# First modulation columns of an adaLN block: product rows with a transpose, or product columns directly

## The chip, the cores and the metric

The kernel runs on one core of one Trainium2 chip. The metric is the device time of one execution in microseconds. Three runs of the kernel before took 1825.55, 1825.82 and 1824.29 us: median 1825.55. Engines are named as in the profile: PE is TensorE's products and PEld its weight loads, DVE is VectorE, ACT is ScalarE, POOL is GpSimd, SP is the engine that issues most DMAs.

## The reference, cut to what matters

A vector `c` of 576 numbers makes six modulation rows of 576 each; the first two (`sa`, `ca`) shift and scale the normalised input ahead of the attention projections. Only that head is touched here.

```python
mod = (_silu(c) @ w_mod).reshape(c.shape[0], 6, 1, -1)
sa, ca, ga, sb, cb, gb = (mod[:, 0], mod[:, 1], mod[:, 2], mod[:, 3], mod[:, 4], mod[:, 5])
h = _layernorm(x, axis=-1) * (1 + ca) + sa
x = x + ga * _A_ref(h, A_wq, A_wk, A_wv, A_wo, A_beta)   # q, k, v = h @ wq, h @ wk, h @ wv; 4 segments of 512 tokens
h = _layernorm(x, axis=-1) * (1 + cb) + sb
x = x + gb * _B_ref(h, B_w_gate, B_w_up, B_w_down)       # SwiGLU, 4608 wide
```

Here x is 2048 x 576, in float32; the attention has 32 heads of 18 and a memory that is carried from segment to segment.

## The kernel before

The kernel works in stages: projections of the four segments of 512 tokens (with the first attention units between them), attention with its output product, and the feed-forward part, which takes about two thirds of the time. In the first stage the order on each engine is set by the scheduler of the tile framework, which may move independent instructions past each other; instructions wrapped in `pin` keep their program order among themselves. From the attention on the order is written out by hand. Every engine works through its own queue in order.

What happens first, all in the first 20 us:

- SP issues the loads: the last 64 rows of the two slices of `w_mod` (`wm[4]`, line 354), then `wm[0]` to `wm[3]` (128 rows each of both slices, line 359) between the four row blocks of the first segment of x (line 311), then four tiles of `wqk` (`wraw`, line 320).
- ScalarE and VectorE make silu(c) as columns (`sga`, lines 362 to 365). VectorE normalises the row blocks of x (lines 251 to 258), with POOL taking the power of the variance.
- The 576 values of c stand in `sga` as four columns of 128 and two of 64 (column 4 holds its values on partitions 0 to 63, column 5 on partitions 64 to 127, and `wm[4]` holds the rows for `ca` on the lower and for `sa` on the upper partitions).
- TensorE makes the two modulation rows (line 380). The stationary operand is `sgb`, each column of `sga` copied 32 times (line 372); the moving operand is a piece of 320 columns of the slice. Four products, one for each half of `ca` and of `sa`, go to four groups of 32 partitions of one bank `pr` and accumulate over the five slices.
- ScalarE takes `pr` out as `row` and adds 1 to the partitions of `ca` (line 383, by the bias `half`). TensorE turns `row` in three transposes into `pc` (line 388, `pcr` in the profile), and VectorE copies its columns to `colv` (lines 392, 393): 128 features x 5 blocks x (scale, shift).
- In between TensorE transposes the normalised x into two banks `pt` (line 263, through `trans_x`), four transposes of 128x128 for each block of 128 features.
- For each of five blocks ScalarE takes `pt` out with scale and shift from `colv`, once rounded (`hh`, line 270) and once in full (`hf`, line 271), and VectorE makes the remainder `hl` (line 272). `hr` holds both for the last 64 features.
- The first three tiles of `wqk` are split by ScalarE (`wqkh`, line 325) and VectorE (`wqkl`, line 326), the others by POOL and VectorE (lines 90, 91).
- TensorE multiplies the first three tiles by `hh`, `hl` and `hr` (`proj3`, line 559, result `pp`), then the others (line 113). ScalarE takes `pp` out (`pf`, `fh`, lines 573, 574), and the keys are transposed for the memory (line 530, `ptk`).
- ScalarE also issues the load of `gat` (line 628), on which its next step waits (line 636).

The lines that lead from `colv` to the first projection:

```python
nc.scalar.activation(hi, pt[:n], AF.Identity, scale=sc[:n], bias=bi[:n])
nc.scalar.activation(f[:n], pt[:n], AF.Identity, scale=sc[:n], bias=bi[:n])
nc.vector.tensor_tensor(lo, f[:n], f32(hi), op=ALU.subtract)
...
for kt, _ in enumerate(trans_in(0)):
    if kt == 0:
        split_qk(2)
...
for kt, t in [(kt, t) for kt in range(3) for t in QKORD[:3]] + [(kt, t) for t in QKORD[:3] for kt in (3, 4)]:
    h, l = wqkh[:, t, kt, :], wqkl[:, t, kt, :]
    for a, b in ((h, hh[kt]), (l, hh[kt]), (h, hl[kt])) if kt < 4 else ((h, hr), (l, hr)):
        nc.tensor.matmul(first[t], lhsT=a, rhs=b, start=(kt == 0 and a is h and b is hh[0]),
                         stop=(kt == 4 and a is l))
```

The constants: `ident` is the 128x128 identity, `ones` is all ones, and `tri` (128x512, made by POOL, line 152) is 0 in its first 384 columns.

Of the kernel before, what the change touches and what calls it, by code (L numbers as in the profile page):

```python
# [7 lines left out]
F32 = mybir.dt.float32  # L8
F32R = mybir.dt.float32r
BF16 = mybir.dt.bfloat16  # L10
AF = mybir.ActivationFunctionType
ALU = mybir.AluOpType
# [3 lines left out]
P = 128  # L16
# [6 lines left out]
L = 512  # L23
# [60 lines left out]
def block(ctx: ExitStack, tc: tile.TileContext, x, wqk, wv, wo, beta, wgu, wgr, wd, c, crow, w_mod, w_mod0, w_mod1, w_modc, xt, out):  # L84
    nc = tc.nc
    def pool(stk, name, bufs=1, **kw):
        return stk.enter_context(tc.tile_pool(name=name, bufs=bufs, reuse_waits="tile", **kw))
# [5 lines left out]
    def chain(*g):  # L93
        for a in g:
            yield from a

    def once(g):
        yield next(g)
# [20 lines left out]
    ident = cst.tile([P, P], F32, tag="ident", name="ident")  # L119
# [3 lines left out]
    ones = cst.tile([P, P], F32, tag="ones", name="ones")  # L123
# [3 lines left out]
    half = cst.tile([P, 1], F32, tag="half", name="half")  # L127
# [22 lines left out]
    tri = vst.tile([P, L], F32, tag="tri", name="tri")  # L150
# [3 lines left out]
    colv = cst.tile([P, 5, 2], F32, tag="colv", name="colv")  # L154
# [90 lines left out]
    def ln_stats(wk, xs, n):  # L245
        st = wk.tile([P, n, 2, 6], F32, tag=f"st{n}", name="st")
        mv = wk.tile([P, n, 2], F32, tag=f"mv{n}", name="mv")
        rs = wk.tile([P, n], F32, tag=f"rs{n}", name="rs")
        for i in range(n):
            for h in range(2):  # L250
                nc.vector.bn_stats(st[:, i, h, :], xs[i][:, 288 * h:288 * h + 288])
            nc.vector.bn_aggr(mv[:, i, :], st[:, i, :, :])
        nc.vector.tensor_scalar(rs, mv[:, :, 1], EPS, None, op0=ALU.add)
        nc.gpsimd.tensor_tensor(rs, rs, mhalf[:, :n], op=ALU.pow)
        return mv, rs

    def xhat(dst, src, mv, rs, i):
        nc.vector.tensor_scalar(dst, src, mv[:, i, 0:1], rs[:, i:i + 1], op0=ALU.subtract, op1=ALU.mult)
# [15 lines left out]
    with ExitStack() as p1:  # L274
# [5 lines left out]
        wk = pool(p1, "wk1", 2)  # L280
        ps = pool(p1, "ps1", 2, space=PSUM)
# [25 lines left out]
        def load_x(s):  # L307
            t = xs[s] = x1.tile([P, 5 * L], F32, tag="x", name=f"x{s}")[:, :4 * D].rearrange("p (a b) -> p a b", b=D)
            for i in range(4):
                r = L * s + P * i  # L310
                nc.sync.dma_start(t[:, i, :], x[r:r + P, :])
                yield
# [5 lines left out]
        def load_qk(t):  # L318
            rq[t] = raw.tile([P, 5, P], F32, tag="wraw", name="wraw", bufs=4)
            nc.sync.dma_start(rq[t], wqk[t])  # L320
# [21 lines left out]
        def trans_x(s, pts, kt, pin):  # L342
            pts[kt] = ps.tile([P, L], F32, tag="t", name="pt")
            for i in transpose_group(pts[kt], lambda i: xs[s][:, i, :], kt):
                pin(i)

        sga = wk.tile([P, 12], F32, tag="sg", name="sg")
        sg = sga[0:96, 6:12]
        with ExitStack() as p0:
            m0 = pool(p0, "m0")  # L350
            wm = {}
            gx = load_x(0)
            wm[4] = m0.tile([P, D], F32, tag="wm4", name="wm4")
            nc.sync.dma_start(wm[4], w_mod1)
            for k in range(4):
                wm[k] = m0.tile([P, 2, D], F32, tag=f"wm{k}", name=f"wm{k}")
                for _ in range(XP[k]):
                    next(gx)
                nc.sync.dma_start(wm[k], w_mod0[k])
            load_qk(0)  # L360

            nc.scalar.activation(sga, cs, AF.Exp, scale=-1.0)
            nc.vector.tensor_scalar(sga, sga, 1.0, None, op0=ALU.add)
            nc.vector.reciprocal(sga, sga)
            nc.vector.tensor_tensor(sga, sga, cs, op=ALU.mult)

            for i in range(4):
                mv, rs = ln_stats(wk, [xs[0][:, i, :]], 1)
                xhat(xs[0][:, i, :], xs[0][:, i, :], mv, rs, 0)

            sgb = wk.tile([P, 6, 32], F32, tag="sgb", name="sgb", bufs=1)
            nc.vector.tensor_copy(sgb, sga[:, 0:6].unsqueeze(2).to_broadcast([P, 6, 32]))
            pr = ps.tile([P, L], F32, tag="s1", name="pr", bufs=3)
            pin = tc.keep_in_program_order
            pt0 = {}
            for k in (4, 0, 1, 2, 3):
                for g in range(4):
                    c0 = 256 * (g % 2)
                    w = wm[4][:, c0:c0 + 320] if k == 4 else wm[k][:, g // 2, c0:c0 + 320]
                    pin(nc.tensor.matmul(pr[32 * g:32 * g + 32, :320], lhsT=sgb[:, k + g // 2 if k == 4 else k, :], rhs=w,  # L380
                                         start=(k == 4), stop=(k == 3)))
            row = wk.tile([P, L], F32, tag="hf", name="row")[:, :320]
            nc.scalar.activation(row, pr[:, :320], AF.Identity, bias=half)
            trans_x(0, pt0, 0, pin)
            pc = ps.tile([P, 3, P], F32, tag="s1", name="pcr", bufs=3)
            for b in range(3):
                n = P if b < 2 else 64
                pin(nc.tensor.transpose(pc[:n, b, :], row[:, 128 * b:128 * b + n], ident))
            trans_x(0, pt0, 1, pin)
            pv = pc.rearrange("p b (s h z) -> p b s h z", s=2, h=2)  # L390
            for h in range(2):
                nc.vector.tensor_copy(colv[:, 2 * h:2 * h + 2, :], pv[:, 0:2, :, h, 0])
            nc.vector.tensor_copy(colv[0:64, 4, :], pv[0:64, 2, :, 1, 0])

        pb = pool(p1, "pb", 2)
        pk = pb.tile([P, 4, D], F32, tag="pk", name="pk", bufs=1)
# [232 lines left out]
        for s in range(NSEG):  # L629
            if s == 0:  # L630
                gp, gw = prep(1), load_wv()
                g = chain(once(gp), once(gw), once(gp), once(gw), once(gp), gw, gp)
            else:
                g = prep(s + 1) if s + 1 < NSEG else iter(())
# [52 lines left out]
    wk = pool(p2, "wk2", 2)  # L687
    opl_ = pool(p2, "op2")
    ps = pool(p2, "ps2", 2, space=PSUM)
# [92 lines left out]
    op = pool(p2r, "op", side="right")  # L782
# [696 lines left out]
    with tc.manual_schedule():  # L1479
# [7 lines left out]
        for u in range(NU + 1):  # L1487
            s, q = divmod(u, 8)
# [25 lines left out]
        ps = pool(p2r, "pst", 2, space=PSUM)  # L1514
# [38 lines left out]
        for i in range(4):  # L1553
            for h in range(2):
                for c in range(WC):
                    n = 8 * i + 4 * h + c
# [28 lines left out]
        ps = pool(p4, "ps4", 1, space=PSUM)  # L1585
# [5 lines left out]
        n, nw = 0, PF  # L1591
# [5 lines left out]
        for t in range(2):  # L1597
            for p in range(NPR):
# [18 lines left out]
                for k in range(14):  # L1617
                    z, m = ZM[k]
# [188 lines left out]
```

## Time and profile before

| | |
|---|---|
| median of three runs | 1825.55 us |
| the profiled execution | 1824.92 us |
| its span, from the first to the last instruction | 1823.2 us |
| mean granted TensorE clock | 0.999 |
| TensorE busy (PE) | 1792.0 us, 98% |
| TensorE weight loads (PEld) | 1522.1 us, 83% |
| VectorE, ScalarE, POOL busy | 81%, 60%, 37% |

Rows of the timeline begin with the start and the duration in microseconds from the span's start; then come the engine, the line, the operation, out<-in, the size, and how many like it were merged into the row. Brackets hold the engine's idle time before it and what ended it. Rows by stretch give the stretch, its length, and each engine's busy time with its instructions. A float32 product stands in the trace as two records, since its operand is split.

### The profile page before, as it was taken

How to read it: one execution, taken by the hardware profiler on the slowest of the kernel's cores; microseconds unless marked ns; L12 is line 12 of the kernel's file. 1: busy time of each engine (PE TensorE's matmuls, PEld its weight loads, DVE VectorE, ACT ScalarE, POOL GpSimd, SP SyncE). 2: the span in 40 equal slices, each digit the busy share in tenths (PEclk: the TensorE clock that was granted, in tenths of full speed). 3: DMA queues.
4: the chain of work that ended last, by engine and by line, in shares of the span. 5: the costliest groups of instructions: out<-in, count | busy, mean ns of one | idle time of the engine just before them, and what ended most of it. 6: DMA issues, size and time to landing. Idle time of an engine off the chain costs nothing.

```text
span 1823.2 us, 31453 instructions
## 1 busy us (share of the span) xinstructions
PE 1792.0 (98%) x10627; PEld 1522.1 (83%) x10627; DVE 1481.7 (81%) x3365; ACT 1086.9 (60%) x2374; POOL 674.1 (37%) x1107
## 2 busy tenths in 40 slices
PE   7999999999999999999999999999999999999999
PEld 4888866777777788888888888888888888888888
DVE  7556388888885799889889889868888888888886
ACT  4333288878775567777777777534544544544542
POOL 2444077775466665756656656300000000000000
PEclk9999999999999999999999999999999999999999
DMA  8768766667556656355455455494333334324331
GB/s 273 258 230 281 258 209 199 194 199 227 166 164 224 209 168 193 128 176 183 134 177 184 115 165 155 154 307 153 107 107 117 96 101 129 103 83 129 107 102 53
DMA packets 146419, 306.26 MB, mean 168 GB/s; under 512 B 30964, under 2 KB 61812, under 8 KB 144468
## 3 DMA queue, kind: packets, MB, share of 16 engines
q1 hardware_dynamic: 135076, 260.19, 46.9%
q10 hardware_dynamic: 11184, 44.07, 6.2%
q8 instruction: 85, 1.39, 0.3%
q14 instruction: 74, 0.61, 0.1%
HBM read 198.69 MB, written 104.94 MB: 167 GB/s over the span
## 4 chain that ended last, share of the span: by engine, by line
PE 84%; DMA 2%; DVE 2%; ACT 2%; POOL 1%; issue 1%; SPq 0%; ACTq 0%; DVEq 0%; POOLq 0%
PE A L1321 24%; PE pd L1440 19%; PE C L1321 12%; PE B L1321 6%; PE av L731 4%; PE s L210 3%; PE s L707 3%; PE pw L841 3%; PE pd L1460 3%; PE pp L113 2%; PE pv L113 2%; PE pn L909 1%; DVE junk L215 1%; PE px L752 1%; ACT Pt L714 1%
## 5 line engine op out<-in xcount | busy, mean ns | idle before, releaser
L1321 PE MATMUL A<-y,wh 128*128 128x512 f32 x1152 | 405.1, 392 | 4.5 <-ACT tb L1350 2.0
L1448 DVE TENSOR_TENSOR acc<-acc,pd 128x576 f32<-128x576 f32 x327 | 245.0, 750 | 78.6 <-PE pd L1440 72.5
L215 DVE CUSTOM_DVE_ANT_0 junk<-s,tri 128x256 bf16<-128x256 f32 (+3 forms) x512 | 221.4, 484 | 60.8 <-PE s L210 46.7
L1440 PE MATMUL pd<-dh,ah 128*128 128x288 f32 x896 | 267.6, 299 | 0.0
L1440 PE MATMUL pd<-dl,ah 128*128 128x288 f32 x896 | 263.9, 295 | 0.0
L1440 PE MATMUL pd<-dh,al 128*128 128x288 f32 x896 | 262.5, 293 | 0.0
L1321 PEld LDWEIGHTS A<-y,wh 128*128 128x128 f32 x1152 | 216.6, 188 | 43.9 <-ACT tb L1350 2.5
L1283 DVE TENSOR_TENSOR wl<-O,wh 128x256 fp32r<-128x256 f32 x504 | 239.1, 478 | 5.5 <-ACT wh L1282 4.8
L1321 PE MATMUL A<-y,wl 128*128 128x512 f32 x576 | 225.0, 391 | 0.0
L714 ACT ACTIVATE Pt<-s 128x512 f32<-128x512 f32 (+1 forms) x352 | 182.7, 558 | 44.3 <-PE s L707 28.0
L1321 PE MATMUL C<-y,wh 128*128 128x512 f32 x576 | 202.7, 393 | 0.0
L1282 ACT CAST wh<-O 128x256 fp32r<-128x256 f32 x504 | 198.2, 405 | 4.4 <-DMA O<-in_wgu_dram 2.5
L1440 PEld LDWEIGHTS pd<-dh,ah 128*128 128x128 f32 x896 | 168.4, 188 | 18.5 <-ACT pd L1416 3.9
L1440 PEld LDWEIGHTS pd<-dl,ah 128*128 128x128 f32 x896 | 169.7, 189 | 16.2
L1386 DVE TENSOR_TENSOR al<-sg,ah 128x512 fp32r<-128x512 f32 x240 | 177.1, 738 | 6.8 <-ACT ah L1385 6.5
L1276 POOL TENSOR_TENSOR O<-O 128x128 f32<-128x128 f32 x280 | 156.4, 592 | 69.8 <-DMA O<-in_wgu_dram 40.9
L1440 PEld LDWEIGHTS pd<-dh,al 128*128 128x128 f32 x896 | 169.2, 189 | 0.0
L1385 ACT CAST ah<-sg 128x512 fp32r<-128x512 f32 x240 | 149.0, 621 | 26.3 <-DVE sg L1345 25.6
L707 PE MATMUL s<-qs,ks 110*128 110x512 f32 (+2 forms) x384 | 143.2, 390 | 4.1 <-ACT Pt L714 1.8
L210 PE MATMUL s<-ks,qs 108*128 108x256 f32 (+3 forms) x512 | 143.8, 334 | 2.6 <-DVE mx L215 2.5
L1321 PEld LDWEIGHTS C<-y,wh 128*128 128x128 f32 x576 | 108.0, 188 | 18.8
L1321 PEld LDWEIGHTS A<-y,wl 128*128 128x128 f32 x576 | 108.3, 188 | 14.9
(389 smaller groups left out, 4063.5 us busy)
## 6 DMA issues: line engine op xcount, KB each, us to landing
wr<-rD SPq DMA_DIRECT2D x216, 112.0 KB
O<-in_wgu_dram SPq DMA_DIRECT2D x36, 512.0 KB
oD<-O ACTq DMA_DIRECT2D x36, 512.0 KB
O<-oD SPq DMA_DIRECT2D x36, 512.0 KB
ks<-kD SPq DMA_DIRECT2D x96, 144.0 KB
O<-in_wgu_dram SPq DMA_DIRECT2D x36, 384.0 KB
qs<-qD SPq DMA_DIRECT2D x64, 192.0 KB
y<-yD SPq DMA_DIRECT2D x11, 1024.0 KB
```

What stands on the lines that cost most here:

```text
L210: nc.tensor.matmul(bank[:, n * (h - h0):n * (h - h0) + n], lhsT=qst[b][0:108, h, 128 * i:128 * i + 128], rhs=kst[b][0:108, h // 2, 0:n], s ...
L215: nc.vector.tensor_tensor_reduce(junk[:, :n], bank[:, n * (h - h0):n * (h - h0) + n], tri[:, L - n:], 1.0, -3e38, op0=ALU.add, op1=ALU.max ...
L707: nc.tensor.matmul(bank[:, n * (g - h):n * (g - h + w)].rearrange("p (a b) -> p a b", a=w), lhsT=kst[u % NB][0:110, g // 2, 128 * j:128 * ...
L714: nc.scalar.activation(pt[:, h:h + per, :n], bank[:, :n * per].rearrange("p (a b) -> p a b", a=per), AF.Exp, scale=SCALE)
L1276: eng.tensor_tensor(o[:, d, i, s_], o[:, a, i, s_], o[:, b, i, s_], op=op)
L1282: nc.scalar.copy(wh, o)
L1283: later.append(lambda: nc.vector.tensor_tensor(wl, o, f32(wh), op=ALU.subtract))
L1321: nc.tensor.matmul(bank, lhsT=a, rhs=b, start=(first and n == 0), stop=(n == 6), skip_group_check=not first)
L1385: nc.scalar.copy(ah, src)
L1386: later.append(lambda: nc.vector.tensor_tensor(al, src, f32(ah), op=ALU.subtract))
L1440: nc.tensor.matmul(pd[:, i, :288], lhsT=a[:, tk], rhs=w, start=(add and k == 0), stop=(k == 2), skip_group_check=not add)
L1448: nc.vector.tensor_tensor(o, o, pd[:, :, :288], op=ALU.add)
```

## The change

The slices become the stationary operand, in pieces of 128 features (the last has 64), and a single column of `sga` is the moving one. Each product gives one column of `pr`, for feature block `b`, half `z` (0 for `ca`, 1 for `sa`) and part `k`. There are six parts: the five slices, and a constant one, made with `ident` as stationary operand and a column of ones (for `ca`) or of zeros from `tri` (for `sa`). The products don't accumulate; VectorE sums the six parts into `colv`. `sgb`, `row`, its evacuation and its three transposes are gone. All products of `pr` are pinned ahead of the transposes of x. That makes 60 products instead of 20, and 2 reductions instead of 3 copies.

```diff
-            sgb = wk.tile([P, 6, 32], F32, tag="sgb", name="sgb", bufs=1)
-            nc.vector.tensor_copy(sgb, sga[:, 0:6].unsqueeze(2).to_broadcast([P, 6, 32]))
-            pr = ps.tile([P, L], F32, tag="s1", name="pr", bufs=3)
+            pr = ps.tile([P, 5, 2, 6], F32, tag="s1", name="pr", bufs=3)
             pin = tc.keep_in_program_order
             pt0 = {}
-            for k in (4, 0, 1, 2, 3):
-                for g in range(4):
-                    c0 = 256 * (g % 2)
-                    w = wm[4][:, c0:c0 + 320] if k == 4 else wm[k][:, g // 2, c0:c0 + 320]
-                    pin(nc.tensor.matmul(pr[32 * g:32 * g + 32, :320], lhsT=sgb[:, k + g // 2 if k == 4 else k, :], rhs=w,
-                                         start=(k == 4), stop=(k == 3)))
-            row = wk.tile([P, L], F32, tag="hf", name="row")[:, :320]
-            nc.scalar.activation(row, pr[:, :320], AF.Identity, bias=half)
+            for k in (5, 4, 0, 1, 2, 3):
+                for z in range(2):
+                    for b in range(5):
+                        n = P if b < 4 else 64
+                        c0 = slice(128 * b, 128 * b + n)
+                        if k == 5:
+                            w, r = ident[:, :n], (tri if z else ones)[:, 0:1]
+                        elif k == 4:
+                            w, r = wm[4][:, c0], sga[:, 4 + z:5 + z]
+                        else:
+                            w, r = wm[k][:, z, c0], sga[:, k:k + 1]
+                        pin(nc.tensor.matmul(pr[:n, b, z, k:k + 1], lhsT=w, rhs=r, start=True, stop=True))
             trans_x(0, pt0, 0, pin)
-            pc = ps.tile([P, 3, P], F32, tag="s1", name="pcr", bufs=3)
-            for b in range(3):
-                n = P if b < 2 else 64
-                pin(nc.tensor.transpose(pc[:n, b, :], row[:, 128 * b:128 * b + n], ident))
             trans_x(0, pt0, 1, pin)
-            pv = pc.rearrange("p b (s h z) -> p b s h z", s=2, h=2)
-            for h in range(2):
-                nc.vector.tensor_copy(colv[:, 2 * h:2 * h + 2, :], pv[:, 0:2, :, h, 0])
-            nc.vector.tensor_copy(colv[0:64, 4, :], pv[0:64, 2, :, 1, 0])
+            nc.vector.tensor_reduce(colv[:, 0:4], pr[:, 0:4], axis=mybir.AxisListType.X, op=ALU.add)
+            nc.vector.tensor_reduce(colv[0:64, 4], pr[0:64, 4], axis=mybir.AxisListType.X, op=ALU.add)
```

The change also renumbers the lines behind it by 4 (line 559 before is 555 now), and the scheduler sets some of the later instructions of the projection stage in another order.

## The prediction

> **What bounds the kernel now.** I read the head of the page first, then busy time by stretch, then the start of the timeline.
>
> ```profile
> span 1823.2 us, 31453 instructions
> PE 1792.0 (98%) x10627; PEld 1522.1 (83%) x10627; DVE 1481.7 (81%) x3365; ACT 1086.9 (60%) x2374; POOL 674.1 (37%) x1107
> ...
> core 0: us, PE busy (x) PEld busy (x) DVE busy (x) ACT busy (x) POOL busy (x), PEclk, DMA share, GB/s
> 0.00:20.00 20.00, 10.19 (x59) 3.81 (x60) 11.81 (x34) 5.48 (x9) 9.28 (x27) 1.00 0.79 283
> 20.00:32.00 12.00, 10.87 (x51) 8.07 (x50) 11.13 (x20) 8.35 (x15) 2.61 (x3) 1.00 0.89 268
> 32.00:40.00 8.00, 7.98 (x41) 6.62 (x42) 7.00 (x18) 4.22 (x9) 0.43 (x1) 1.00 0.89 326
> 40.00:60.00 20.00, 20.00 (x110) 17.09 (x109) 10.58 (x15) 7.24 (x15) 14.38 (x13) 1.00 0.85 289
> 60.00:100.00 40.00, 40.00 (x237) 34.79 (x237) 24.79 (x72) 13.32 (x26) 7.14 (x12) 1.00 0.64 199
> ```
>
> TensorE bounds the whole: 1792.0 of 1823.2 us busy. It is idle for half of the first 20 us, has 1.1 us of idle in 20 to 32, and from 32 to 100 us it never stops. So whatever delays the first projection product is not won back later: a microsecond lost at the start is a microsecond at the end, less what little the gaps before 32 us take up. The changed lines all lie in the first 17 us; their chain is this (start, duration, engine):
>
> ```profile
> 5.05 0.30 POOL L152 TENSOR_SCALAR_AFFINE_SELECT tri<-tri 128x128 f32<-128x128 f32 x1
> ...
> 8.39 1.30 PE L380 MATMUL pr<-wm,sgb 128*32 128x320 f32 x8 [0.39 <-DMA wm<-in_w_mod_dram]
> 10.56 1.29 PE L380 MATMUL pr<-wm,sgb 128*32 128x320 f32 x8 [0.87 <-DMA wm<-in_w_mod_dram]
> 12.72 1.30 PE L380 MATMUL pr<-wm,sgb 128*32 128x320 f32 x8 [0.87 <-DMA wm<-in_w_mod_dram]
> 14.18 1.30 PE L380 MATMUL pr<-wm,sgb 128*32 128x320 f32 x8 [0.16 <-DMA wm<-in_w_mod_dram]
> 15.41 1.12 PE L263 MATMUL pt<-ident,x 128*128 128x128 f32 x4
> 15.61 0.53 ACT L383 ACTIVATE row<-pr,half 128x320 f32<-128x320 f32 x1 [11.46 <-PE pr L380]
> 16.04 0.72 ACT L325 CAST wqkh<-wraw 128x640 fp32r<-128x640 f32 x1
> 16.32 0.61 PE L388 MATMUL pcr<-ident,row 128*128 128x128 f32 x3
> 16.76 0.60 PE L263 MATMUL pt<-ident,x 128*128 128x128 f32 x4
> 16.97 0.23 DVE L392 COPY colv<-pcr 128x4 f32<-128x4 f32 x2 [1.63 <-PE pcr L388]
> 17.16 0.78 ACT L270 ACTIVATE hh<-pt,colv 128x512 fp32r<-128x512 f32 x1 [0.41 <-DVE colv L392]
> 17.84 0.71 ACT L325 CAST wqkh<-wraw 128x640 fp32r<-128x640 f32 x1
> 17.99 0.50 PE L559 MATMUL pp<-hh,wqkh 128*128 128x512 f32 x1 [0.63 <-ACT hh L270]
> ```
>
> Now DMA ends the waits: each group of products takes 1.30 us and the last four slices arrive 1.5 to 2.2 us apart, so TensorE keeps pace. From the last slice (14.18) to the first `hh` (17.16) it is 2.98 us. Each group has 4 products in the code and 8 records here: a float32 product is two records, each with its own weight load; a transpose is one.
>
> **The change, part by part.** Removed: the `sgb` copy, the row evacuation (0.53), three transposes (0.61) and the copies (0.23). Of these, evacuation, transposes and copies stand between 15.48 and 17.16; but the 8 `pt` transposes stay, and 4 of them must also precede `hh`.
>
> Added on TensorE: per slice 10 products (8 with 128 columns of weights, 2 with 64), so 20 records, each with a weight load and one moving column; and 10 products ahead for the constant. What one costs is the disputed price, since no row has one moving column. The nearest rows are short products, where loads follow each other without waiting for the data that streams:
>
> ```profile
> 302.36 0.53 PEld L210 LDWEIGHTS s<-ks,qs 108*128 108x128 f32 x4
> ...
> 623.23 0.33 PEld L1440 LDWEIGHTS pd<-dl,ah 128*128 128x128 f32 x1
> 623.47 0.33 PEld L1440 LDWEIGHTS pd<-dh,al 128*128 128x128 f32 x1
> ...
> 624.30 0.19 PEld L1321 LDWEIGHTS B<-y,wh 128*128 128x128 f32 x1
> ```
>
> Four loads of 128 columns span 0.53 us and the last takes 0.19, so they start (0.53 - 0.19) / 3 = 0.113 us apart. One load takes 0.33 where the others take 0.19: that stretch has the half clock, as the next fence shows. There loads start 0.24 us apart, behind 288 moving columns each, so 0.24 is an upper end for half clock and 0.113 a lower one. I take 0.11 at full and 0.22 at half clock, since the load's duration grows by 0.14, more than a whole 0.11; half of it for 64 columns, in proportion. A slice then costs 16 x 0.22 + 4 x 0.11 = 3.96 us at half and 1.98 at full clock, against 1.30 now.
>
> Which clock holds there:
>
> ```profile
> core 0: us, PE busy (x), PEclk, DMA share, GB/s
> 6.30:9.70 3.40, 2.59 (x16) 1.00 1.00 392
> ...
> 13.10:16.50 3.40, 3.24 (x21) 1.00 1.01 389
> ...
> 617.30:620.70 3.40, 1.61 (x10) 1.00 0.67 268
> 620.70:624.10 3.40, 3.40 (x11) 0.50 0.53 197
> 624.10:627.50 3.40, 3.40 (x20) 1.00 0.85 263
> ```
>
> The column PEclk prints 1.00 before its first record, but the transposes of the same shape say otherwise: four take 1.12 us at 15.41 and 0.60 at 16.76. So the first 16.5 us run at half clock, and full clock comes after a stretch that is nearly full (3.24 of 3.40 busy), not after one with 2.59. The same shows at 620.7: after 1.61 busy comes 0.50, after 3.40 busy again 1.00.
>
> Would a stream of weight loads with one column each count as busy? The profile has no such stream. Streaming, it does almost nothing: one column in the 0.11 to 0.22 us that 128 could fill. I take it that it does not count (odds about 3 to 2), and the half clock stays. By the Trainium skill, "TensorE: Matmul & The Clock Gate", Part 1, the clock is gated to half by default and released by about 3.4 us of sustained activity; that agrees with the stretches above, and leaves open what counts as activity.
>
> The places in TensorE's and ScalarE's queues, of before and of the change. TensorE before, from the fourth slice (wm_262) on; pp is the first projection:
>
> ```order
> L380 MATMUL pr<-wm_262,sgb 32x320 x4
> L380 MATMUL pr<-wm_265,sgb 32x320 x4
> L263 MATMUL pt<-ident,x_255 128x128 x4
> L388 MATMUL pcr<-ident,row 128x128 x2
> L388 MATMUL pcr<-ident,row 64x128
> L263 MATMUL pt<-ident,x_255 128x128 x4
> L559 MATMUL pp<-hh_366,wqkh 128x512
> ```
>
> TensorE now, from its first product (a slice's rows stand twice, once for each half z; they are shown once):
>
> ```order
> L385 MATMUL pr<-ones,ident 128x1 x4
> L385 MATMUL pr<-ones,ident 64x1
> L385 MATMUL pr<-tri,ident 128x1 x4
> L385 MATMUL pr<-tri,ident 64x1
> L385 MATMUL pr<-sg,wm_252 128x1 x4
> L385 MATMUL pr<-sg,wm_252 64x1
> ...
> L385 MATMUL pr<-sg,wm_265 128x1 x4
> L385 MATMUL pr<-sg,wm_265 64x1
> L263 MATMUL pt<-ident,x_255 128x128 x8
> L555 MATMUL pp<-hh_397,wqkh 128x512 x2
> ```
>
> Everything of `pr` stands ahead of the transposes, and the constant's second half waits for `tri` (5.35). ScalarE before, from the evacuation, then now:
>
> ```order
> L383 ACTIVATE row<-pr,half 128x320
> L325 CAST wqkh<-wraw 128x640
> L270 ACTIVATE hh_366<-pt,colv 128x512
> L325 CAST wqkh<-wraw 128x640
> L271 ACTIVATE hf<-pt,colv 128x512
> ```
>
> ```order
> L270 ACTIVATE hh_397<-pt,colv 128x512
> L325 CAST wqkh<-wraw 128x640 x2
> L271 ACTIVATE hf<-pt,colv 128x512
> ```
>
> The first cast, which now runs at 16.04 in an idle stretch, gets behind `hh` and waits with it; behind it wait VectorE's first `wqkl` and TensorE's first projection product. In the rows above `hh`, cast, `hf` start 0.6 to 0.7 us apart, so all that follows `hh` is 0.7 later.
>
> The sum, at half clock. The `tri` products: 5.35 + 1.98 = 7.33. Five slices: 7.33 + 5 x 3.96 = 27.1; no arrival binds, the last is at 14.18 and its group begins at 23.2. Four transposes at 1.12: 28.2. The two reductions on VectorE run beside the transposes (VectorE's two copies took 0.23; without this cover they would cost about 0.3). So `hh` starts at about 28.3 instead of 17.16: 11.1 us. The cast: 0.7. The first projections then run partly at half clock: about 0.5. Against it, a wait of TensorE behind the first projection may take up part:
>
> ```profile
> 31.26 0.23 ACT L636 ACTIVATE gat<-gat 128x32 f32<-128x32 f32 x1 [1.76 <-DMA gat<-in_beta_dram]
> ...
> 32.02 0.66 PE L530 MATMUL ptk<-ident,pf 128*128 128x128 f32 x4 [0.86 <-ACT pf L573]
> ```
>
> These 0.86 us hang on the load of `gat`, which ScalarE issues after its evacuations, so it moves too; I credit 0.3. Together 11.1 + 0.7 + 0.5 - 0.3 = 12.0 us.
>
> The rest of the order moves little: SP's `wqk`, `xb` and `wv` loads trade a few places (one `wv` load goes behind three `kD` stores), POOL's order is unchanged, and in the next two blocks some score products shift by a few rows; I give this +-1 us, by the size of the wait just shown.
>
> The profiled execution took 1824.92 us (span 1823.2 and 1.7 around it), 0.63 under the median of 1825.55. 1824.92 + 12.0 = 1836.9 for it, 1837.5 for the median.
>
> **The rivals.** First, the stream counts as busy and the clock rises. From 5.35 on TensorE is never idle, so the stretch 6.3 to 9.7 is full and full clock holds from 9.7. Then 7.33 to 9.7 does 0.6 of a slice, the other 4.4 cost 1.98 each: 18.4; four transposes at 0.60: 19.0; `hh` is 1.9 late, with the cast 2.6, and 1828.1 for the median. For it: the profile counts such records as busy back to back. Against it: hardly a column moves. It lies within 0.2% (3.65 us, about what a measurement of this kernel can tell from no change), unless the stretches fall up to 3.4 us later, which adds up to 1.7 (half of it): 1829.8. Chance 0.32.
>
> Second, on the other side, not slower: one-column products overlap their loads better than the rows of L210, at about 0.06 us a record. Then 20 records take 1.2 us, under the 1.46 between the last two slices; the last group ends at 15.4, the transposes at 16.5, `hh` begins 0.55 earlier, and the cast's 0.7 makes it even: 1825.7. It decides below about 0.07 us a record. By the Trainium skill, the same page, "Wait — 56ns, not 53.3ns?", products with few columns start no closer than about 25 ns; if only that bound, the result would be this one. The 0.113 of L210 speaks against it. Chance 0.08.
>
> **How the numbers follow.** Half clock 0.58, full clock 0.32, even 0.08, anything else 0.02. Likeliest 1837.5; its own range is 1834 to 1841 (0.24 instead of 0.22 a record adds 1.8, the order 1, the missing recovery 0.3). The range reaches down over the full-clock case, less 1 for the order: 1827 to 1841. Slower: 0.58 and a third of 0.32, with the remainder: 0.70; same: 0.25; faster: 0.05.
>
> **What would show it.** In the profile after: L385's loads 0.22 us apart up to about 27 us, with transposes at 1.12 for four, and `hh` near 28. If loads are 0.11 apart from about 10 us on, the clock is the step that failed; if they are at 0.06, the load's price. If `hh` is late but the end is not, then the claim fails that nothing is won back after 32 us.

## The result and the profile after

The changed kernel takes 1840.03 us (median of 6 runs, 1838.23 to 1842.01) beside 1825.37 us for the kernel before (6 runs on the same chip): a ratio of 1.0081, 95% interval 1.0069 to 1.0094, 14.7 us slower. The prediction was 1837.5, within 1827 to 1841. The profiled execution took 1842.01 us, the slowest of the six; its span is 17.1 us longer than the one before. That is 2.4 more than the medians say; a wait in this one execution, shown below, put more than that on it.

The head of the page of after:

```profile
span 1840.3 us, 31601 instructions
PE 1813.9 (99%) x10704; PEld 1547.7 (84%) x10704; DVE 1482.6 (81%) x3363; ACT 1086.2 (59%) x2373; POOL 672.3 (37%) x1107
```

Its busy time by stretch (for each engine busy us and instructions):

```profile
core 0: us, PE busy (x) PEld busy (x) DVE busy (x) ACT busy (x) POOL busy (x), PEclk, DMA share, GB/s
0.00:20.00 20.00, 17.16 (x82) 16.85 (x82) 9.40 (x26) 1.50 (x2) 8.88 (x27) 1.00 0.75 273
20.00:32.00 12.00, 11.37 (x51) 10.36 (x50) 1.59 (x4) 2.74 (x5) 0.00 (x0) 1.00 0.00 0
```

From 20 to 32 us the whole core now waits for TensorE: VectorE has 1.59 us of work where it had 11.13, POOL and the DMAs none. TensorE itself is nearly full in the first 32 us (28.5 us busy, 21.1 before), and the page calls it 99% busy: its share of busy time rose while the kernel became slower.

The chain of the first 31 us, from the timeline (start, duration, engine, then what ended the idle time before it):

```profile
5.00 2.17 PE L385 MATMUL pr<-tri,ident 128*128 128x1 f32 x10 [1.31 <-POOL tri L151]
7.10 21.08 PE L385 MATMUL pr<-sg,wm 128*128 128x1 f32 x100
28.11 1.97 PE L263 MATMUL pt<-ident,x 128*128 128x128 f32 x8
28.22 0.21 DVE L388 TENSOR_REDUCE colv<-pr 128x8 f32<-128x48 f32 x1 [13.28 <-PE pr L385]
29.26 0.78 ACT L270 ACTIVATE hh<-pt,colv 128x512 fp32r<-128x512 f32 x1 [25.18 <-PE pt L263]
29.94 1.34 ACT L325 CAST wqkh<-wraw 128x640 fp32r<-128x640 f32 x2
30.70 1.42 PE L555 MATMUL pp<-hh,wqkh 128*128 128x512 f32 x2 [0.63 <-ACT wqkh L325]
```

The 100 records of the slices take 21.08 us, 0.21 us each from the first to the last, with nothing between them that TensorE waits for: the last slice had landed at 14.18 before, and its products end at 28.2. The first `hh` starts 12.1 us later (29.26, 17.16 before), the first projection product 12.7 later (30.70, 17.99 before). The transposes take 0.25 us each (1.97 for 8), the half-clock price (1.12 for 4 before). So the clock is at half through the whole stream, which the profile calls full, as busy time by stretch shows (PEclk prints 1.00 ahead of its first record here too; that record, the step to full clock, stands at 34.9 us):

```profile
core 0: us, PE busy (x), PEclk, DMA share, GB/s
7.00:14.00 7.00, 7.00 (x35) 1.00 1.02 405
...
21.00:28.00 7.00, 7.00 (x35) 1.00 0.00 0
```

What the lag becomes later is read from the same instruction in both timelines, the first product of the next step (L113) and the first score product behind the projection stage; of before, then of after:

```profile
32.43 0.48 PE L113 MATMUL pp<-hh,wqkh 128*128 128x512 f32 x1
...
229.17 0.40 PE L707 MATMUL s<-qs,ks 110*128 110x512 f32 x1
```

```profile
44.73 0.48 PE L113 MATMUL pp<-hh,wqkh 128*128 128x512 f32 x1
...
48.91 0.66 PE L526 MATMUL ptk<-ident,pf 128*128 128x128 f32 x4 [0.67 <-DVE pk L530]
...
89.87 0.50 PE L113 MATMUL pp<-hr,wqkh 128*128 128x512 f32 x1 [0.98 <-DVE hr L460]
...
243.68 0.40 PE L703 MATMUL s<-qs,ks 110*128 110x512 f32 x1
...
280.53 0.67 PE L703 MATMUL s<-qs,ks 110*128 110x512 f32 x1 [2.56 <-DMA qs<-mr]
```

The lag is 12.3 us at the end of the first projections and 14.5 at the end of the stage. Two stops stand in between where TensorE never stopped before (0.67 and 0.98 us). At 280.5 ends a wait of 2.56 us for `qs`, 0.52 before, and then comes a stretch at half clock; behind it the lag is 18.3 us (the first L210 product there starts at 284.84, 266.50 before):

```profile
277.20:280.60 3.40, 0.84 (x7) 1.00 0.92 229
280.60:284.00 3.40, 3.40 (x17) 0.50 1.00 349
```

### The profile page after: what moved, and what is told of

It reads as the page before. It is cut to its first block, busy times and chain, and to the rows that moved or that the text cites. A ratio compares the mean times of both kernels' runs of the same rounds, so it can differ in the third digit from the quotient of the medians.

```text
span 1840.3 us, 31601 instructions
## 1 busy us (share of the span) xinstructions
PE 1813.9 (99%) x10704; PEld 1547.7 (84%) x10704; DVE 1482.6 (81%) x3363; ACT 1086.2 (59%) x2373; POOL 672.3 (37%) x1107
## 4 chain that ended last, share of the span: by engine, by line
PE 91%; ACT 2%; DVE 2%; DMA 2%; issue 1%; POOL 1%; SPq 0%; ACTq 0%; DVEq 0%; POOLq 0%
PE A L1317 25%; PE pd L1436 19%; PE C L1317 12%; PE B L1317 6%; PE av L727 4%; PE pp L113 4%; PE s L210 4%; PE s L703 3%; PE pv L113 3%; PE pw L837 3%; PE pd L1456 3%; PE pr L385 1%; ACT Pt L710 1%; DMA xb<-in_x_dram 1%; PE pn L905 1%
## 5 line engine op out<-in xcount | busy, mean ns | idle before, releaser
L210 PE MATMUL s<-ks,qs 108*128 108x256 f32 (+3 forms) x512 | 144.0, 334 | 3.5 <-DVE mx L215 3.1
```

The costliest lines, as they stand in the source:

```text
L210: nc.tensor.matmul(bank[:, n * (h - h0):n * (h - h0) + n], lhsT=qst[b][0:108, h, 128 * i:128 * i + 128], rhs=kst[b][0:108, h // 2, 0:n], s ...
```

## The experiments

The theory (A): the clock rises, and stays up, on time in which TensorE streams columns; a weight load with one column behind it counts as none, so the stream keeps the clock at half and its records cost 0.21 us instead of 0.11. The rivals: something else holds the clock down in these 30 us (the start of the program, the loads themselves), or it is not the head but the later order that costs. Two short theories concern what is left: why 12.3 us become 14.5. Times of the first four kernels stand beside 1825.69 us for before (12 runs), those of the second four beside 1824.50 (15 runs). The lags of all are in one table behind the experiments.

**Dense products ahead of the stream** (e1_dense). Five filler products of 512 columns, whose result nobody reads (the kernel has the loop in a helper; it is written out here):

```diff
+fb_ = ps.tile([P, L], F32, tag="p", name="fill", bufs=3)
+for _ in range(5):
+    pin(nc.tensor.matmul(fb_.rearrange("p (a b) -> p a b", b=P), lhsT=ident, rhs=ones.unsqueeze(1).to_broadcast([P, 4, P]), start=True, stop=True))
 for k in (5, 4, 0, 1, 2, 3):
```

> The change, with five dense float32 products of 512 columns (identity times ones, result unused) ahead of all products of pr, about 8.5 us of solid TensorE work from 1.5 us on. Theory A: the price of a one-column record is a weight load at the granted clock, and a stream of such records counts as idle, so the clock rises during the dense products and falls again 3.4 to 6.8 us after them. Then some L385 loads start 0.105 us apart and later ones 0.21 again; the stream ends at 25 to 28.5 us, and the time is 1837 to 1840. Rival B: the stream holds the clock once it is up; all loads behind the dense products are 0.105 apart, the stream ends near 20, and the time is about 1832. Rival C: the clock has no part in the price; loads stay 0.21 apart though the clock is up, the stream ends near 31, and the time is 1842 or more.

Measured: 1839.57 us (4 runs), ratio 1.0070, interval 1.0053 to 1.0087. TensorE and its weight loads (PEld) in the timeline:

```profile
1.53 7.34 PE L377 MATMUL fill<-ones,ident 128*128 128x512 f32 x10 [1.53 <-POOL half L128]
...
10.98 18.70 PE L390 MATMUL pr<-sg,wm 128*128 128x1 f32 x100
...
6.81 0.34 PEld L377 LDWEIGHTS fill<-ones,ident 128*128 128x128 f32 x1 [0.52 <-issue]
7.42 0.19 PEld L377 LDWEIGHTS fill<-ones,ident 128*128 128x128 f32 x1 [0.27 <-issue]
```

Its busy time by stretch:

```profile
core 0: us, PE busy (x), PEclk, DMA share, GB/s
7.20:9.80 2.60, 2.60 (x15) 1.00 0.98 378
10.90:13.90 3.00, 3.00 (x27) 1.00 1.01 412
14.00:18.00 4.00, 4.00 (x21) 0.50 0.80 293
```

This run decides the clock. The dense products raise it at 7.2 us (a load takes 0.19 instead of 0.34), so the start of the program does not hold it down. The one-column records that follow start 0.11 us apart (27 in 3.0 us) until 14.0; then the clock falls back to half in the middle of the stream, with TensorE "busy" for 4.00 of 4.00 us and no pause, and the same records start 0.21 us apart (a block of ten takes 1.19 us at 10.98 and 2.10 at 14.91). The stream counts as idle. By the Trainium skill, "TensorE: Matmul & The Clock Gate", Part 1, the clock falls back to half after an idle window of about 3.4 us; the trace agrees, with dense work until 8.9 and the fall at 14.0, and adds that records without streamed columns make such a window. (Later in these kernels less than a whole idle window was enough; see the last section.) The time gains nothing, since the filler puts the constant's products off until 8.7 and the full clock lasts for about 27 of the 100 records; the stream ends at 29.7, later than the 25 to 28.5 that I expected.

**One column that is 128 columns** (e7_wide). Every product moves its column 128 times; the next product overwrites all but the first, and the sums stay the same. For that `pr` is laid out in the order of the products (`prw` is the whole bank, `j` a product's place in that order); the lines that do this are left out here:

```diff
-pin(nc.tensor.matmul(pr[:n, b, z, k:k + 1], lhsT=w, rhs=r, start=True, stop=True))
+j = 10 * order_k.index(k) + 5 * z + b
+pin(nc.tensor.matmul(prw[:n, j:j + P], lhsT=w, rhs=r.to_broadcast([r.shape[0], P]), start=True, stop=True))
```

> Each of the 60 products moves 128 equal columns instead of one; the product after it overwrites all but the first of them, and the sums stay the same. Theory A (the clock rises on time in which the array streams columns, and time spent on loading weights does not count): at half clock a record stays at 0.21 us, because 128 columns stream beside the next load, so the stream starts alike at 7.1 us; now it counts as activity, full clock comes between 10.6 and 14 us, the rest of the records take 0.11 us, the stream ends between 18 and 21.5 instead of 28.2, hh at 19.5 to 22.5 instead of 29.26, 7 to 10 us earlier. Rival B (what holds the clock down is the weight loads themselves, or the start of the program): the clock stays at half until 34, hh at 29 to 30. Rival C (loads and streaming don't overlap here): 0.42 us a record at half clock, hh later than 32. The whole time follows the head only within some 2 us, since the order of the later instructions shifts too: A 1830 to 1834, B 1840, C 1844 or more.

Measured: 1841.41 us (4 runs), ratio 1.0089, interval 1.0075 to 1.0102. TensorE, its loads (PEld), then VectorE and one later stop of TensorE in the timeline:

```profile
7.63 15.66 PE L388 MATMUL pr<-sg,wm 128*128 128x128 f32 x100
23.22 1.09 PE L263 MATMUL pt<-ident,x 128*128 128x128 f32 x8
...
7.63 1.78 PEld L388 LDWEIGHTS pr<-sg,wm 128*128 128x128 f32 x8 [0.33 <-DVE rs L253]
9.63 0.29 PEld L388 LDWEIGHTS pr<-sg,wm 128*64 128x64 f32 x2 [0.22 <-issue]
10.14 1.28 PEld L388 LDWEIGHTS pr<-sg,wm 128*128 128x128 f32 x10 [0.22 <-issue]
...
24.96 0.71 DVE L623 TENSOR_TENSOR wvl<-wvraw,wvh 128x576 fp32r<-128x576 f32 x1
25.59 0.20 DVE L391 TENSOR_REDUCE colv<-pr 128x8 f32<-128x48 f32 x1
...
119.50 0.39 PE L230 MATMUL pmt<-ident,mc 128*32 128x128 f32 x1 [7.44 <-POOL mc L224]
```

A holds and the other two fall: with the same loads at the same place and work in every column, the loads of 128 columns go from 0.21 us apart (8 in 1.78, the last of them 0.33 long) to 0.11 at 10 us, and they keep that pace to the end. The head gains less than I expected, in two places. Each block of 10 records takes 1.45 us and not 1.1: at full clock 0.31 us pass between the last load of 128 columns and the first of 64, and again between the last of 64 and the next of 128 (10.92 to 11.23 and 11.29 to 11.60 us). So the stream ends at 23.2 and not by 21.5. And VectorE, which has other work ahead in this kernel's order, sums only at 25.59, so `hh` starts at 25.89: 3.4 us earlier than in the changed kernel, not 7 to 10. I had bounded the later order with 2 us; here TensorE stops for 7.44 us from 112 us on, for `mc` from POOL, and the head's gain is gone at the end of the stage.

**The same, with TensorE kept busy from the start** (e8_wide_fill). One filler of 512 columns in the pause ahead of `tri`:

```diff
 for z in range(2):
+    if k == 5 and z:
+        fb_ = ps.tile([P, L], F32, tag="p", name="fill", bufs=3)
+        pin(nc.tensor.matmul(fb_.rearrange("p (a b) -> p a b", b=P), lhsT=ident, rhs=ones.unsqueeze(1).to_broadcast([P, 4, P]), start=True, stop=True))
```

> As the run with 128 moving columns, with one dense product of 512 columns (a filler whose result nobody reads) between the two groups of the constant's products, where TensorE waits 1.3 us for tri. Theory A: no pause of TensorE from 1.5 us on, so full clock comes at 7.2 instead of 10.6 to 14, the 100 records of the slices take 10.7 us and end near 18, hh at 18.7 to 19.5. Rival B: half clock until 34, hh at 29 to 30. By A the time is 1828 to 1832, still above that of before, because 10.7 us of records after 7.2 end later than the last slice's products did (15.5).

Measured: 1843.45 us (4 runs), ratio 1.0099, interval 1.0085 to 1.0113. In the timeline:

```profile
5.98 1.42 PE L391 MATMUL pr<-tri,ident 128*128 128x128 f32 x10
7.43 14.60 PE L391 MATMUL pr<-sg,wm 128*128 128x128 f32 x100
...
25.96 0.20 DVE L394 TENSOR_REDUCE colv<-pr 128x8 f32<-128x48 f32 x1
```

The clock is up from 6 us on (1.42 us for 10 records, 2.69 in the run before), as A says, and all 100 records run at full clock, at 0.146 us and not the 0.107 I had put: the stream ends at 22.0. The sum then waits for VectorE until 25.96. The head is 3.0 us better than in the changed kernel; the order behind it costs more than that (TensorE stops for `mc` here too, for 7.3 us at 115), and the time misses my 1828 to 1832. Both runs tell of the clock; their whole times tell of an order that shifted with them.

**Half of the products** (e2_half). The second half's products (z = 1) are left out, in the slices and in the constant, and its columns get the sums of the first:

```diff
-                for z in range(2):
+                for z in range(1):
```

> The change with half of its products: the shift columns are left out and the scale's sums are written in their place (the result is not the reference's). Later instructions stand in the order of the change. Theory A: time goes by the number of records at 0.21 us; 60 instead of 120, the last slice's arrival (14.18) now nearly binds, the stream ends near 17 and the first hh is at about 18.0, 11.2 us earlier than with the change. What the changed order costs later (2.2 us between 33 us and the end of the projections) stays: about 1829. Rival: the head is late for another reason than the count (a wait, instruction supply), and the gain is under 5 us: 1835 or more. Rival on the order: the 2.2 us come from running late and not from the order, then they go too: about 1827.

Measured: 1831.57 us (9 runs), ratio 1.0028, interval 1.0017 to 1.0038. In the timeline:

```profile
7.71 10.57 PE L385 MATMUL pr<-sg,wm 128*128 128x1 f32 x50 [4.01 <-DVE sg L365]
...
19.36 0.78 ACT L270 ACTIVATE hh<-pt,colv 128x512 fp32r<-128x512 f32 x1 [15.07 <-PE pt L263]
```

Half the records take half the time (10.57 instead of 21.08 us), `hh` comes 9.9 us earlier, and the median falls by 8.5: the price is per record, and the head's lag reaches the end of the kernel. The stop ahead of `hr` stands here too (0.95 us at 79.5), and the lag grows from 3.0 to 5.4 by the end of the stage: a head that is 9 us earlier brings the same growth, with both stops in it (the other one is 0.46 us at 38.9). The head gains less than the 11.2 us that I expected, since the stream waits until 7.71 for `sg` and ends at 18.2 instead of near 17, and the time is 2.6 us above my 1829.

**The changed kernel once more** (e0_again), nothing edited.

> The changed kernel once more, nothing edited. Theory 1: the loss in the head (first hh at 29.26 us, 12.1 later than before) and the short waits behind it (0.67 us at 48.2, 0.98 at 88.9) come from the instructions' order, so they stand again, hh at 29.1 to 29.7 and a lag of 14 to 14.6 us at the end of the projection stage (about 229 us of before), while the wait of 2.56 us for qs at 278 and the half clock from 280.6 to 284 belong to that one run; the span then lies near 1838. Rival: the short waits belong to that run too; then the lag at the end of the projection stage is near 12.5 and the short waits are elsewhere. Median 1838 to 1841 by both.

Measured: 1838.88 us (4 runs), ratio 1.0080, interval 1.0064 to 1.0096; span 1835.0 us. In the timeline:

```profile
29.19 0.78 ACT L270 ACTIVATE hh<-pt,colv 128x512 fp32r<-128x512 f32 x1 [24.91 <-PE pt L263]
...
90.41 0.50 PE L113 MATMUL pp<-hr,wqkh 128*128 128x512 f32 x1 [0.97 <-DVE hr L460]
```

Busy time by stretch, the two stretches that were shown of after:

```profile
277.20:280.60 3.40, 3.04 (x30) 1.00 0.81 239
280.60:284.00 3.40, 3.40 (x35) 1.00 1.00 355
```

The head stands again to 0.1 us, and so does the stop ahead of `hr`; the lag at the end of the stage is 15.0. The long wait at 278 and the half clock behind it are gone. So those 15 us belong to the change, and what came at 280 to that one execution. Its span is shorter than I expected, only 11.9 us above that of before. The lag, by the same product in both timelines, is 14.7 us at 600 us of before, 13.4 at 616 and 12.0 at 630: before has a pause and a half-clock stretch of its own at 617 to 624 us (in the prediction's rows) and this run has no half clock, which makes about half of the 2.7; the other half before loses ahead of it, between 600 and 616.

**`hr` ahead of the statistics on VectorE** (e5_hr). The remainder `hr` of the second segment and the `bn_stats` behind it are pinned in that order, as they ran before:

```diff
-nc.vector.tensor_tensor(hr[64:128], f[0:64], f32(hr[0:64]), op=ALU.subtract)
+i = nc.vector.tensor_tensor(hr[64:128], f[0:64], f32(hr[0:64]), op=ALU.subtract)
+if s == 1:
+    pin(i)
...
-nc.vector.bn_stats(st[:, i, h, :], b[:, 288 * h:288 * h + 288])
+j = nc.vector.bn_stats(st[:, i, h, :], b[:, 288 * h:288 * h + 288])
+if s == 2 and i >= 2:
+    pin(j)
```

> The change, with one pair of VectorE's instructions held in program order: hr of segment 1 (line 464 of before) ahead of the bn_stats of the third and fourth row block of segment 2, which wait for a load. Theory A: the 1.0 us stop of TensorE at 88.9 us, where it waits for hr while VectorE waits for xb, is gone, and the lag against before at the end of the projection stage is 13.2 instead of 14.5 us: 1838.7. Rival: the stop only moves, to the loads or to segment 2's projections, and the lag stays 14.5: 1840.

Measured: 1839.07 us (4 runs), ratio 1.0069, interval 1.0052 to 1.0086. In the timeline:

```profile
89.32 0.39 PE L113 MATMUL pp<-hl,wqkh 128*128 128x512 f32 x1
89.56 0.40 PE L113 MATMUL pp<-hr,wqkh 128*128 128x512 f32 x1
```

The stop is gone: the product with `hr` follows 0.24 us behind its neighbour. From the head to the end of the stage the lag grows by 1.2 us instead of 2.2 and 2.4 in the two profiles of the changed kernel; 0.2 to 0.4 of that is the other stop, which is 0.45 us here (0.67 and 0.81 there). In the medians a microsecond is below what they can tell; the place of this part is shown, its size in the whole time is not. The lag at the end of the stage is 13.9 us where I expected 13.2.

**The transposes ahead of the last slice** (e6_trans). All eight transposes of x go ahead of the last slice's products:

```diff
 for k in (5, 4, 0, 1, 2, 3):
+    if k == 3:
+        trans_x(0, pt0, 0, pin)
+        trans_x(0, pt0, 1, pin)
...
-trans_x(0, pt0, 0, pin)
-trans_x(0, pt0, 1, pin)
```

> The change, with the eight transposes of x ahead of the last slice's products instead of behind them. Theory A: the stream ends where it ended plus nothing (the same work), and only the two reductions stand between it and the first hh, so hh comes at about 28.5 + 1.7 - 1.7, that is 0.8 us earlier than with the change (29.26); the clock stays at half till after the stream, since 1.7 us of transposes do not fill a 3.4 us stretch. Time about 1839.2. Rival: transposes of that length are enough to raise the clock; then the last slice takes 2.1 instead of 4.2 and hh comes near 26.

Measured: 1837.30 us (4 runs), ratio 1.0060, interval 1.0045 to 1.0075. In the timeline:

```profile
25.68 4.11 PE L388 MATMUL pr<-sg,wm 128*128 128x1 f32 x20
...
30.06 0.78 ACT L270 ACTIVATE hh<-pt,colv 128x512 fp32r<-128x512 f32 x1 [14.50 <-DVE colv L389]
30.74 0.71 ACT L325 CAST wqkh<-wraw 128x640 fp32r<-128x640 f32 x1
30.89 0.79 PE L556 MATMUL pp<-hh,wqkh 128*128 128x512 f32 x1 [1.11 <-ACT hh L270]
```

`hh` is 0.8 us later, not earlier: all eight transposes are now ahead of it, where it needs four. The last slice's 20 records still take 4.11 us, so 2 us of transposes here don't raise the clock; whether they count at all stays open. In this order the first cast is done before `hh`, and the first projection product starts 0.83 us behind `hh`, as before the change, instead of 1.44: the cast that got behind `hh` costs 0.61 us. The median is nevertheless only 11.6 us above that of before, where the changed kernel had 14.7 and 14.4. The profile doesn't show this: the lag at the end of the stage is 14.3 us, and the span is 0.4 us longer than that of e0_again. The intervals overlap, and no gain is taken from it.

**The kernel before, with filler products in its pauses** (f4_before_fill): the one version that the runs pointed to as better than both. `dense(n, w)` issues n products of 128 x w columns, w being 4 where it isn't given:

```diff
+dense(2)
 for k in (4, 0, 1, 2, 3):
     for g in range(4):
...
+    if k in {4: 1, 0: 2, 1: 2, 2: 1}:
+        dense(1, {4: 1, 0: 2, 1: 2, 2: 1}[k])
```

> The kernel before, with dense filler products (ident as weights, a broadcast column, nobody reads their result) in the pauses of the first 14 us: two of 512 columns ahead of all, and one each of 128, 256, 256 and 128 columns ahead of the slices' products. Theory A: full clock comes between 7.2 and 10.6 us instead of 16.55, the last slice's 8 records take 0.65 instead of 1.30 us and the transposes half as long, so hh starts at 16.0 to 16.4 instead of 17.16 and the time falls by about 1 us (1824 to 1825 beside 1825.5; no more than the measurement can tell). Rival: the pauses that are left let the clock fall back, or a filler still runs when a slice lands: hh at 17.2 to 18, time the same or 1 us more.

Measured: 1824.86 us (11 runs), ratio 1.0002, interval 0.9993 to 1.0011: no difference that can be told. TensorE and ScalarE in the timeline:

```profile
14.28 0.74 PE L385 MATMUL pr<-wm,sgb 128*32 128x320 f32 x8 [0.28 <-DMA wm<-in_w_mod_dram]
...
15.09 1.55 ACT L325 CAST wqkh<-wraw 128x640 fp32r<-128x640 f32 x2 [10.99 <-DMA wraw<-in_wqk_dram]
16.55 0.52 ACT L390 ACTIVATE row<-pr,half 128x320 f32<-128x320 f32 x1
```

Its TensorE by stretch:

```profile
13.90:17.30 3.40, 1.83 (x15) 1.00 0.90 345
17.30:20.70 3.40, 3.19 (x12) 0.50 0.84 246
```

The last slice's products do take 0.74 us instead of 1.30. But in this order two casts stand ahead of `row` on ScalarE, so `row` comes at 16.55 instead of 15.61, and `hh` starts at 18.12, 1.0 us later than before. From `row` to `hh` it is 1.57 us, 1.55 before, so the 1.0 us is the late `row`. TensorE pauses for it and the clock falls back at 17.3, as the rival says; that comes too late to delay `hh`. My expectation failed by an order that I had not counted. With `row` kept ahead of the casts it was not tried.

The lags against the kernel before (starts of the same instruction, us):

| kernel | first `hh` | first projection product | first L113 | end of the stage (last L113) |
|---|---|---|---|---|
| before (start) | 17.16 | 17.99 | 32.43 | 229.04 |
| after | +12.1 | +12.7 | +12.3 | +14.5 |
| e0_again | +12.0 | +12.6 | +12.6 | +15.0 |
| e1_dense | +13.6 | +13.6 | +13.4 | +12.8 |
| e2_half | +2.2 | +2.8 | +3.0 | +5.4 |
| e5_hr | +12.5 | +13.1 | +12.7 | +13.9 |
| e6_trans | +12.9 | +12.9 | +12.6 | +14.3 |
| e7_wide | +8.7 | +8.7 | +8.1 | +16.0 |
| e8_wide_fill | +9.1 | +9.1 | +11.2 | +20.1 |
| f4_before_fill | +1.0 | +1.0 | +0.6 | +0.8 |

## Why the prediction was right, point by point

- *The clock.* That a stream of loads with one column does not count as busy was the disputed step, at odds of 3 to 2. The stream ran at half clock for its whole 21 us; e1_dense shows the clock falling in the middle of it and e7_wide shows it rising when the columns are there. The first rival (full clock from 9.7 us) is refuted. An estimate of what the clock is worth: at the 1.19 us of a block of ten that e1_dense shows at full clock, the 100 records would take 11.9 us instead of 21.1, so about 9 of the 12 us of the head are the half clock.
- *The price.* 0.22 us for a load of 128 columns at half clock was 0.21. Half of it for 64 columns was wrong: the four records of 64 columns cost as much, on average, as the others, so a slice takes 4.2 us, not 3.96. The two loads of such a product start only 0.06 us apart, but 0.35 us pass ahead of the first and 0.25 behind the second (8.55 to 9.21 us of after), where it is 0.21 between loads of 128 columns. The stream ends at 28.2 instead of 27.1, `hh` starts at 29.3 instead of 28.3. The second rival (0.06 us a record) is far off: at full clock it is 0.11.
- *The cast.* 0.7 predicted, 0.61 by e6_trans.
- *Projections at half clock and recovery.* +0.5 and -0.3 were given. The lag goes from 12.7 at the first product to 12.3 at the next step, so the sum of the two is -0.4 instead of +0.2. In total the head costs 12.3 us where 12.0 stood, since a `hh` that is 1.0 later is offset by this and by the cast. That the three nearly cancel is luck.
- *The later order.* This is the term that was mis-sized: +-1 us by one stop of the profile, and +2.2 us measured (+2.4 in the second profile). The two stops are 1.65 of it (1.78), where the prediction had the size of a single one. In e5_hr, which removes the larger, the growth is 1.2. In e1_dense, whose later order differs, no stop stands ahead of `hr`, and the lag shrinks from 13.4 to 12.8, while e2_half, with a head 9 us earlier and both stops, has the growth; so it is the order and not the late head that makes this term. The stops are not all of it: e6_trans has none ahead of `hr` either, and its lag grows by 1.7. The rest was not taken apart. The 2.5 us between 1837.5 and the median are this term and the 0.3 of the head.
- *What goes on to the end.* 14.5 to 15.0 us of lag behind the projection stage, 14.7 in the medians (14.4 for e0_again): that nothing is won back after the head holds. In the table, too, the lag at the end of the stage is within 1.2 us of the difference of the medians for every kernel but e6_trans (14.3 beside 11.6). Single executions scatter more behind the stage: the 17.1 of the two spans has the wait for `qs` and the half clock at 280 in it, which the second profile of the same kernel does not, and its 11.9 has the pauses of before.

## What to carry to other kernels

Turning a row product into column products makes each of them a weight load, and a float32 product two of them: count the records and price them by loads that follow each other, not by the columns they move. A stretch that the profile shows as fully busy can still be idle for the clock, so price it at half clock unless columns are streaming in it. And when an edit in a scheduled stage moves the estimated times, look at what the scheduler reorders later: here that was 2 of 15 us, and in three of the experiments (e7_wide, e8_wide_fill, f4_before_fill) it was as large as what they were meant to win.

## What the runs showed of the hardware

- A stretch of 100% busy time (100 records in 21.08 us, no pause) leaves the clock at half; the same records start 0.11 us apart while an earlier dense stretch still keeps it up, for 5 us after the last dense product (e1_dense, 8.9 to 14.0 us).
- Loads of 64 columns save nothing in such a chain: 10 records with two of 64 columns take 2.1 us at half clock, 10 x 0.21, and 1.19 at full, 10 x 0.12. The short loads lie close together (0.06 us); the changes of width take up what they save.
- 128 moving columns beside each load cost nothing for loads of 128 columns (0.21 us apart at half clock, 0.11 at full, as with one column), and raise the clock; the block of 10 takes 1.45 us then, not the 1.19 of one column, by longer gaps at the changes of width (e7_wide).
- Single half-clock stretches of 3.4 us come and go between executions of one kernel behind a pause of 1.8 to 2.6 us (before at 620.7, after at 280.6 and 639.0, none in e0_again behind the head). With time cut into stretches of 3.413 us from the first record of the clock on, TensorE was busy for 2.04 us or less in each stretch ahead of a fall to half, in all ten traces and apart from the fall inside the stream of e1_dense; the least busy stretch that no fall followed had 1.72 us (e2_half at 626.9). So a pause shorter than the whole stretch is enough. How much of the 4 to 7 us by which runs of one kernel differ is theirs was not measured.
